# A squared-ReLU feed-forward layer on one core: the loads of w1 move from GpSimd's DMA queue to ScalarE's and SyncE's

## The chip, the cores and the metric

The kernel runs on one core of one Trainium2 chip. The metric is the device time of one execution in microseconds (us). The kernel before took 299.13 us, the median of 4 runs (298.64 to 300.1).

## The reference

```python
B, S, D, F = 1, 2048, 576, 4608      # all bf16
def reference(x, w1, b1, w2, b2):
    h = jnp.einsum("bsd,df->bsf", x, w1) + b1
    r = jnp.where(h > 0, h, 0)
    h = r * r
    return jnp.einsum("bsf,fd->bsd", h, w2) + b2
```

Two matrix products with a squared ReLU between them. The hidden dimension F is 36 tiles of 128; the model dimension D = 576 is four tiles of 128 and a rest of 64, or nine slices of 64. The 2048 rows of x are worked on in four blocks of 512.

## The kernel before, in words

**Stage A** makes the hidden layer, transposed, block by block of x. Since D is nine slices of 64, TensorE's 128 rows are used as two halves: one hidden tile contracts on rows 0 to 63 and another one on rows 64 to 127. So the 36 hidden tiles are taken in 18 *pairs* (`pairs`, line 81). The weights lie in SBUF as `w1h`: the first tile of each pair on partitions 0 to 63 (the *lower half*, h = 0), the second on 64 to 127 (the *upper half*, h = 1). A pair costs 18 matmuls (line 179, `a_part`), nine for each half, and then for each half one ScalarE instruction (line 163: bias and ReLU, PSUM to the SBUF tile `r`, of which there are four buffers) and one VectorE instruction (line 165: the square), together `evac_h`.

**Stage B** (from line 285) multiplies the hidden layer by w2, tile by tile of 128 rows of x, and stores the result. TensorE goes from A to B without a pause.

**The start.** `w1h` is large, so the loads come in the order of need.

- The first four hidden tiles (the *quads*, `qn`, and the rest rows, `qr`) are computed with 128 rows of contraction at once, for block 0 only, while `w1h` is on its way. SyncE and ScalarE each issue two tiles of x and two quads (lines 101 to 108). TensorE transposes x by itself (line 146), VectorE and ScalarE copy the transposes from PSUM to SBUF (lines 137, 139, 151), and line 194 multiplies them with the quads. Line 219 adds the rest rows `qr`. The four results lie in four PSUM banks (`bk0`) until lines 163 and 165 evacuate them (lines 223 to 226).
- Then block 0 goes over the other 16 pairs in groups of four (G = 4): *group one* is pairs 2 to 5, *group two* pairs 6 to 9, *group three* 10 to 13, *group four* 14 to 17. Pairs 0 and 1 of `w1h` are not needed before block 1.
- Group one is treated apart: its halves are loaded in two parts, even and odd slices (`w1_first`, line 121), and TensorE goes over the four pairs with the first five slices of each (lines 260 to 262) before it does the other four (lines 263 to 266). There are 8 PSUM banks: the four of `bk0` and those of the first two pairs fill them, and the third pair waits for banks that the evacuation of `bk0` frees.
- `load_w1` (line 97) loads one half of some pairs. In the kernel before, SyncE issues all lower halves and GpSimd all upper halves (lines 122 to 127 and 234): group one in two parts (320 KB and 256 KB), then one transfer of 576 KB for each further group, then 288 KB for pairs 0 and 1. GpSimd also loads the rest rows (line 113) and b1 (line 116). The small copy in line 120 makes GpSimd wait until the first tile of x is there.
- Behind w1, SyncE issues the DMA transposes of x for the blocks 1 to 3 (`load_xT`, line 232), then b2 and parts of w2. `finish_xT` (lines 255 and 256) copies two slices of a transposed block on VectorE; that of block 1 stands in the program behind pair 14 of block 0.

**What sets the order.** The schedule is manual: each engine runs its instructions, DMA issues included, in the order of the program. So a DMA issue on ScalarE that has to wait, or that takes long, holds up ScalarE's copies and evacuations behind it. The framework puts in the semaphores. In the trace, the DMAs from SyncE and ScalarE share eight completion semaphores, which go round in program order, and GpSimd's DMAs eight others; a DMA that reuses a semaphore is issued only after the DMA that had it last has landed.

Of the kernel before, what the change touches and what calls it, by code (L numbers as in the profile page):

```python
# [11 lines left out]
BF16 = mybir.dt.bfloat16  # L12
# [5 lines left out]
def kernel(  # L18
# [9 lines left out]
    nc = tc.nc  # L28
    P = 128
    H = 64  # L30
    x2 = x.flatten_outer_dims()
    out2 = out.flatten_outer_dims()
    S, D = x2.shape
    F = w1.shape[1]
    FH = F // 2
    G = 4
# [3 lines left out]
    NH = D // H  # L40
    DM = NC * P
# [8 lines left out]
    const = ctx.enter_context(tc.tile_pool(name="const", bufs=1))  # L50
# [18 lines left out]
    def early(n):  # L69
        at[0] += n  # L70
        assert at[0] <= NFT * D
        return w2_sb[:, at[0] - n:at[0]]
# [5 lines left out]
    xs = early(RT * D).rearrange("p (j c) -> p j c", c=D)  # L78
    qn = early(NC * 4 * P).rearrange("p (c f) -> p c f", c=NC)
    qr = early(2 * P)  # L80
# [10 lines left out]
    def load_x(eng, j):  # L91
        eng.dma_start(out=xs[:, j, :], in_=x_view[:, j, :])
# [4 lines left out]
    def load_w1(eng, h, j0, n, cs):  # L97
        f0 = pairs[j0][h] * P
        eng.dma_start(out=w1h[h * H:(h + 1) * H, cs, j0 * P:(j0 + n) * P], in_=w1_rows[:, cs, f0:f0 + n * P])  # L99
# [7 lines left out]
    load_x(nc.sync, 2)  # L107
    load_x(nc.scalar, 3)

    ident = const.tile([P, P], BF16, name="ident")  # L110
    make_identity(nc, ident[:])
    for h in range(2):
        nc.gpsimd.dma_start(out=qr[h * H:(h + 1) * H, :], in_=w1[DM:D, 2 * h * P:2 * (h + 1) * P])
    b1_rows = const.tile([P, P], BF16, name="b1_rows")
    nc.gpsimd.memset(b1_rows[:], 0.0)
    nc.gpsimd.dma_start(out=b1_rows[0:NFT, :], in_=b1.rearrange("(ft p) -> ft p", p=P))


    seen = const.tile([P, 1], BF16, name="seen")
    nc.gpsimd.tensor_copy(out=seen[:], in_=xs[:, 0, 0:1])  # L120
    w1_first = ((slice(0, 9, 2), slice(1, 8, 2)), (slice(1, 8, 2), slice(0, 9, 2)))
    for part in range(2):
        for h, eng in enumerate((nc.sync, nc.gpsimd)):
            load_w1(eng, h, 2, G, w1_first[h][part])
    for m in range(1, 4):
        for h, eng in enumerate((nc.sync, nc.gpsimd)):
            load_w1(eng, h, 2 + G * m, G, slice(0, NH))

    ones = nc.const_aps.tensor(1.0, [P, SB], BF16)
    wps = bank("wps")  # L130
# [4 lines left out]
    def copy_psum(eng, dst, src):  # L135
        if eng is nc.scalar:
            nc.scalar.copy(out=dst, in_=src)  # L137
        else:
            nc.vector.tensor_copy(out=dst, in_=src)  # L139

    def transpose_chunks(half, cs, engs):
        tps = [psum.tile([P, HALF], BF16, name="tp", tag="bank") for c in cs]
        for i in range(2):
            for c, tp in zip(cs, tps):
                d0 = c * P if c < NC else D - P
                nc.tensor.transpose(tp[:, i * P:(i + 1) * P], xs[:, 2 * half + i, d0:d0 + P], ident[:])  # L146
        cols = slice(half * HALF, (half + 1) * HALF)
        for c, tp, eng in zip(cs, tps, engs):
            copy_psum(eng, xT[0][:, c if c < NC else 7, cols], tp[:])
            if c == NC:  # L150
                nc.vector.tensor_copy(out=xT[0][0:H, 8, cols], in_=tp[H:P, :])
# [39 lines left out]
    def full_mm(half, c):  # L191
        cols = slice(half * HALF, (half + 1) * HALF)
        for q in range(4):
            nc.tensor.matmul(bk0[q][:, cols], lhsT=qn[:, c, q * P:(q + 1) * P], rhs=xT[0][:, c, cols],  # L194
                             start=(half == 0 and c == 0), stop=False, skip_group_check=True)
# [4 lines left out]
    full_mm(0, 0)  # L200
    transpose_chunks(0, (2,), (A,))
    full_mm(0, 1)
    transpose_chunks(0, (3,), (V,))
    full_mm(0, 2)
    transpose_chunks(1, (0, 1), (V, A))
# [2 lines left out]
    full_mm(1, 0)  # L208
    transpose_chunks(1, (2,), (A,))
    full_mm(1, 1)  # L210
    transpose_chunks(1, (3,), (V,))
    nc.tensor.transpose(b1T_ps[:], b1_rows[:], ident[:])
    full_mm(1, 2)
# [17 lines left out]
        for i in range(2):  # L231
            nc.sync.dma_start_transpose(out=xT[b][:, i * NC:(i + 1) * NC, :], in_=x2[rows, i * H:i * H + DM])

    for h, eng in enumerate((nc.sync, nc.gpsimd)):
        load_w1(eng, h, 0, 2, slice(0, NH))
    for b in range(1, NSB):
        load_xT(b)
    w2_view = w2_dram.rearrange("(ft p) d -> p ft d", p=P)
# [106 lines left out]
```

## Time and profile before

| | |
|---|---|
| median of 4 runs | 299.13 us |
| the profiled execution, its own time | 298.77 us |
| its span, first to last instruction | 297.0 us |
| TensorE matmuls, busy | 286.6 us (96%) |
| ScalarE, VectorE, GpSimd, busy | 94.9, 79.5, 8.1 us |
| HBM read, written | 11.94 MB, 2.36 MB |
| share of the chain by line: L179, L305, w1h transfers | 44%, 42%, 6% |

The page has, for each engine, the time in which it was busy; the span in 40 slices of 7.4 us each with busy tenths, TensorE's granted clock and the DMA rate; the DMA queues (q1 is SyncE's, q10 ScalarE's, q0 GpSimd's); and the chain of work that ended last, followed back from the last instruction. In lists of instructions the columns are start, duration, engine, line, operation, what it writes and reads, shapes and count, and in brackets the idle time ahead of it and who ended it. A matmul's own duration (376 ns) is longer than the distance from one to the next, because they are pipelined. In lists of DMA issues the last number is the time from the issue to the landing.

### The profile page before, as it was taken

The page shows a single profiled execution, that of the slowest core. Times are in us where ns is not written, and L with a number is a line of the kernel's source. Part 1 is how long each engine was busy: PE and PEld are TensorE (multiplying, and loading weights), DVE is VectorE, ACT ScalarE, POOL GpSimd, SP SyncE. Part 2 cuts the span into 40 slices and gives each one's busy share as a digit, 9 for nine tenths or more (in the row PEclk, how much of TensorE's full clock was granted, in tenths as well). Part 3 has the DMA queues.
Part 4 walks back from the last instruction along what each step waited for, and adds up shares of the span by engine and source line. Part 5 has one row for each costly group of instructions (what it writes and reads, how often), then busy time and mean ns, then how long its engine had stood idle before and what let it go on. Part 6 is the DMA issues. An engine that isn't in the chain of part 4 may idle for free.

```text
span 297.0 us, 4817 instructions
## 1 busy us (share of the span) xinstructions
PE 286.6 (96%) x2068; PEld 136.0 (46%) x2079; DVE 79.5 (27%) x196; ACT 94.9 (32%) x151; POOL 8.1 (3%) x19
## 2 busy tenths in 40 slices
PE   7958999999999999999999999999999999999995
PEld 3743444444444444444445444444444444444454
DVE  1541445445444454444440011000111111111111
ACT  2462666666666666666650000000000000000000
POOL 8200000000000000000000000000000000000000
PEclk9997999999999999999999999999999999999999
DMA  7999999200030000600000010000000000000000
GB/s 214 264 253 173 191 201 314 74 2 2 0 121 0 2 1 10 231 2 0 2 0 3 18 20 20 20 22 20 20 20 22 20 20 20 22 20 20 20 22 21
DMA packets 25925, 18.01 MB, mean 61 GB/s; under 512 B 14516, under 2 KB 25216, under 8 KB 25904
## 3 DMA queue, kind: packets, MB, share of 16 engines
q1 hardware_dynamic: 24416, 14.42, 19.9%
q0 software_dynamic: 912, 2.73, 3.6%
q10 hardware_dynamic: 576, 0.56, 0.6%
q8 instruction: 16, 0.26, 0.4%
q14 instruction: 5, 0.04, 0.0%
HBM read 11.94 MB, written 2.36 MB: 48 GB/s over the span
## 4 chain that ended last, share of the span: by engine, by line
PE 91%; DMA 7%; SPq 0%; issue 0%; DVE 0%
PE ph L179 44%; PE po L305 42%; DMA w1h<-in_w_dram 6%; PE pc L291 5%; DMA w_sb<-in_x_dram 1%; SPq L99 0%; DVE o_sb L307 0%
## 5 line engine op out<-in xcount | busy, mean ns | idle before, releaser
L163 ACT ACTIVATE r<-ph,b1T 128x512 bf16<-128x512 f32 x144 | 90.8, 686 | 54.8 <-PE ph L179 53.4
L179 PE MATMUL ph<-w_sb,w1h 64*128 64x512 bf16 x936 | 103.2, 380 | 4.5 <-DMA w1h<-in_w_dram 4.5
L179 PEld LDWEIGHTS <-w1h 64*128 64x128 bf16 x1260 | 64.3, 95 | 78.3 <-DMA w1h<-in_w_dram 5.8
L305 PE MATMUL po<-w_sb,hT 128*128 128x512 bf16 x423 | 92.9, 379 | 0.5
L305 PEld LDWEIGHTS <-hT 128*128 128x128 bf16 x432 | 42.2, 98 | 51.2 <-issue 0.4
L165 DVE TENSOR_TENSOR hT<-r 128x512 bf16<-128x512 bf16 x108 | 46.0, 426 | 61.2 <-ACT r L163 61.1
L307 DVE TENSOR_TENSOR o_sb<-po,b_bc 128x512 bf16<-128x512 f32 (+2 forms) x17 | 11.2, 660 | 116.7 <-PE po L305 109.7
L179 PE MATMUL ph<-xT,w1h 64*128 64x512 bf16 x324 | 35.1, 376 | 0.0
L305 PE MATMUL po<-w_sb,w1h 128*128 128x512 bf16 (+2 forms) x178 | 31.2, 336 | 0.1
L305 PEld LDWEIGHTS <-w1h 128*128 128x128 bf16 x180 | 16.2, 98 | 15.3
L165 DVE TENSOR_TENSOR w1h<-r 128x512 bf16<-128x512 bf16 x36 | 15.3, 426 | 19.6 <-ACT r L163 19.6
L291 PE MATMUL pc<-hT,w_sb 128*64 128x512 bf16 x108 | 15.7, 379 | 0.0
L291 PEld LDWEIGHTS <-w_sb 128*64 128x64 bf16 x144 | 8.1, 110 | 7.6 <-issue 0.4
L291 PE MATMUL pc<-w1h,w_sb 128*64 128x512 bf16 x36 | 7.9, 379 | 0.0
L293 ACT ACTIVATE oc<-pc,b2T 128x512 bf16<-128x512 f32 x2 | 1.4, 688 | 13.7 <-PE pc L291 13.7
L194 PE MATMUL ph<-w_sb 128*128 128x256 bf16 x32 | 4.5, 272 | 1.1 <-DMA w_sb<-in_w_dram 0.8
L301 DVE COPY o_sb<-oc 128x64 bf16<-128x64 bf16 x16 | 2.8, 172 | 9.4 <-DMA oc<-oc 9.4
L99 POOL DMA_DIRECT2D w1h<-in_w_dram x6 | 4.3, 716 | 0.0
L139 DVE COPY w_sb<-tp 128x256 bf16<-128x256 bf16 x6 | 1.7, 290 | 7.3 <-PE tp L146 7.3
L194 PEld LDWEIGHTS <-w_sb 128*128 128x128 bf16 x32 | 2.8, 97 | 1.6 <-DMA w_sb<-in_w_dram 1.3
L133 PE MATMUL wps<-const-bfloat16-1.0 128*128 128x512 bf16 x6 | 2.7, 623 | 0.8 <-PEq L329 0.8
L137 ACT COPY w_sb<-tp 128x256 bf16<-128x256 bf16 x4 | 1.5, 372 | 3.7 <-PE tp L146 3.6
(29 smaller groups left out, 15.5 us busy)
## 6 DMA issues: line engine op xcount, KB each, us to landing
w_sb<-in_w_dram SPq DMA_DIRECT2D x6, 864.0 KB, 6.4
out_dram<-o_sb SPq DMA_DIRECT2D x15, 144.0 KB, 1.7
w1h<-in_w_dram SPq DMA_DIRECT2D x3, 576.0 KB, 21.0
w1h<-in_w_dram POOLq DMA_DIRECT2D x3, 576.0 KB, 12.6
w1h<-in_w_dram SPq DMA_DIRECT2D x1, 320.0 KB, 7.4
w1h<-in_w_dram POOLq DMA_DIRECT2D x1, 320.0 KB, 7.5
w_sb<-in_x_dram ACTq DMA_DIRECT2D x2, 144.0 KB, 4.0
w_sb<-in_x_dram SPq DMA_DIRECT2D x2, 144.0 KB, 3.7
```

Source lines behind the costliest of these rows:

```text
L99: eng.dma_start(out=w1h[h * H:(h + 1) * H, cs, j0 * P:(j0 + n) * P], in_=w1_rows[:, cs, f0:f0 + n * P])
L133: nc.tensor.matmul(wps[:], lhsT=ones[:, 0:P], rhs=ones[:], start=(i == 0), stop=(i == NWARM - 1))
L137: nc.scalar.copy(out=dst, in_=src)
L139: nc.vector.tensor_copy(out=dst, in_=src)
L163: nc.scalar.activation(out=r[:], in_=bk[:], func=ACT.Relu, bias=b1T[:, ft:ft + 1], scale=1.0)
L165: nc.vector.tensor_tensor(out=hT_of(b, ft), in0=r3, in1=r3, op=ALU.mult)
L179: nc.tensor.matmul(bk[h][:], lhsT=w1h[rows, c, j * P:(j + 1) * P], rhs=xT[b][rows, place(h, c), :], start=(i == 0), stop=(i == NH - 1))
L194: nc.tensor.matmul(bk0[q][:, cols], lhsT=qn[:, c, q * P:(q + 1) * P], rhs=xT[0][:, c, cols], start=(half == 0 and c == 0), stop=False, ski ...
L291: nc.tensor.matmul(pc[h * H:(h + 1) * H, :], lhsT=w2(ft, DM, D), rhs=hT_of(2 * pr + h, ft), start=(ft == 0), stop=(ft == NFT - 1))
L301: nc.vector.tensor_copy(out=o_sb[:, DM:D], in_=o_tr[pr][:, jj, h * H:(h + 1) * H])
L305: nc.tensor.matmul(po[:, 0:e - a], lhsT=hT_of(b, ft)[:, jj, :], rhs=w2(ft, a, e), start=(ft == 0), stop=(ft == NFT - 1))
L307: nc.vector.tensor_tensor(out=o_sb[:, a:e], in0=po[:, 0:e - a], in1=b2_bc[:, a:e], op=ALU.add)
```

## The change

GpSimd no longer loads w1 or the rest rows. ScalarE's queue takes the upper halves of groups one and two, in three DMAs that stand between its copies in program order: the odd slices of group one right after its first four loads, the even slices after its second copy of a transpose, and group two after its last copy. All else goes to SyncE: the rest rows, the lower halves, and both halves of groups three and four and of pairs 0 and 1, one after the other. The copy in line 120 goes away. The bytes that are loaded and the computation are the same.

```diff
@@ after load_x(nc.scalar, 3) @@
+    def load_rest(eng, h):
+        eng.dma_start(out=qr[h * H:(h + 1) * H, :], in_=w1[DM:D, 2 * h * P:2 * (h + 1) * P])
+
+    load_rest(nc.sync, 0)
+    w1_first = ((slice(0, 9, 2), slice(1, 8, 2)), (slice(1, 8, 2), slice(0, 9, 2)))
+    load_w1(nc.scalar, 1, 2, G, w1_first[1][0])
+    load_w1(nc.sync, 0, 2, G, w1_first[0][0])
+    load_rest(nc.sync, 1)
+    load_w1(nc.sync, 0, 2, G, w1_first[0][1])
+
     ident = const.tile([P, P], BF16, name="ident")
     make_identity(nc, ident[:])
-    for h in range(2):
-        nc.gpsimd.dma_start(out=qr[h * H:(h + 1) * H, :], in_=w1[DM:D, 2 * h * P:2 * (h + 1) * P])
...
-    seen = const.tile([P, 1], BF16, name="seen")
-    nc.gpsimd.tensor_copy(out=seen[:], in_=xs[:, 0, 0:1])
-    w1_first = ((slice(0, 9, 2), slice(1, 8, 2)), (slice(1, 8, 2), slice(0, 9, 2)))
-    for part in range(2):
-        for h, eng in enumerate((nc.sync, nc.gpsimd)):
-            load_w1(eng, h, 2, G, w1_first[h][part])
-    for m in range(1, 4):
-        for h, eng in enumerate((nc.sync, nc.gpsimd)):
-            load_w1(eng, h, 2 + G * m, G, slice(0, NH))
...
     transpose_chunks(0, (2,), (A,))
     full_mm(0, 1)
+    load_w1(nc.scalar, 1, 2, G, w1_first[1][1])
     transpose_chunks(0, (3,), (V,))
...
     transpose_chunks(1, (2,), (A,))
     full_mm(1, 1)
+    load_w1(nc.scalar, 1, 2 + G, G, slice(0, NH))
+    load_w1(nc.sync, 0, 2 + G, G, slice(0, NH))
     transpose_chunks(1, (3,), (V,))
...
-    for h, eng in enumerate((nc.sync, nc.gpsimd)):
-        load_w1(eng, h, 0, 2, slice(0, NH))
+    for j0, n in ((2 + 2 * G, G), (2 + 3 * G, G), (0, 2)):
+        for h in range(2):
+            load_w1(nc.sync, h, j0, n, slice(0, NH))
     for b in range(1, NSB):
         load_xT(b)
```

## The prediction

> **What bounds the kernel now.** I read the chain that ended last first. TensorE is at its start and end; between lies one transfer, from 4.96 to 23.36 us, and nothing else is as long.
>
> ```profile
> 4.96 18.39 DMA w1h<-in_w_dram
> 23.36 0.05 issue
> 23.40 130.06 PE ph L179 x1188
> 153.47 15.66 PE pc L291 x144
> ```
>
> After it TensorE runs to the end without a hole, so what can be won lies ahead of 23.4 us. Next, the timeline from 0 to 40 us, at the DMA issues, ScalarE's start and the matmuls of line 179:
>
> ```profile
> 2.15 0.46 ACTq L92 DMA_DIRECT2D w_sb<-in_x_dram  x1
> 2.63 1.28 ACT L137 ACT_TABLE_LOAD   x1 [2.63 <-issue]
> ...
> 4.84 0.60 PE L194 MATMUL ph<-w_sb 128*128 128x256 bf16 x4
> 5.04 0.37 ACT L137 COPY w_sb<-tp 128x256 bf16<-128x256 bf16 x1 [0.66 <-PE tp L146]
> ...
> 10.61 2.42 ACT L163 ACTIVATE r<-ph,b1T 128x512 bf16<-128x512 f32 x4 [1.47 <-PE ph L219]
> ...
> 11.01 8.06 PE L179 MATMUL ph<-w_sb,w1h 64*128 64x512 bf16 x72 [0.22 <-DMA w1h<-in_w_dram]
> ...
> 23.40 16.97 PE L179 MATMUL ph<-w_sb,w1h 64*128 64x512 bf16 x140 [4.33 <-DMA w1h<-in_w_dram]
> ```
>
> The 72 matmuls of the first group start at 11.01. The pace of a pair is 1.943 us (ScalarE's pairs of line 163 at 31.12, 33.07, 35.01), so a matmul costs 1.943/18 = 0.108 us and the second group could start at 11.01 + 72 x 0.108 = 18.78. It starts at 23.40: a **gap of 4.62 us**. Which half is late? The issues around 5.3 us, with their time to landing:
>
> ```profile
> w1h<-in_w_dram SPq DMA_DIRECT2D x1, 576.0 KB, 18.4
> w1h<-in_w_dram POOLq DMA_DIRECT2D x1, 576.0 KB, 10.3
> ```
>
> The upper half of the second group (GpSimd) lands at 5.11 + 10.3 = 15.4, the lower (SyncE) at 4.96 + 18.4 = 23.4. The queues from 12 to 20 us (packets, MB, share of 16 engines; q0 is GpSimd's, q1 SyncE's) say why:
>
> ```profile
> q0 software_dynamic: 439, 1.61, 79.0%
> q1 hardware_dynamic: 436, 0.44, 26.0%
> ```
>
> As many packets of each queue, but GpSimd's are nearly four times as large: its groups three and four pass SyncE's group two. Last, the stretches, whose last three figures are TensorE's granted clock, the DMA share and GB/s:
>
> ```profile
> 3.00:6.00 3.00, 2.28 (x20) 1.55 (x18) 1.07 (x4) 1.66 (x3) 2.86 (x6) 1.00 1.01 298
> 12.00:20.00 8.00, 7.07 (x66) 5.72 (x63) 3.58 (x9) 4.64 (x9) 0.00 (x0) 1.00 1.06 258
> 24.00:28.00 4.00, 4.00 (x26) 1.53 (x22) 0.43 (x1) 1.26 (x2) 0.00 (x0) 0.57 1.24 185
> ```
>
> The third line's clock of 0.57: the gap also costs (1 - 0.57) x 4 = 1.7 us. Cross-check: 1188 matmuls x 0.108 = 128.2, the chain has 130.06: 1.8 us, taken.
>
> **Gain if the gap goes:** 4.62 + 1.8 = 6.4 us.
>
> **Part 1, order of arrival.** Up to the second group go x and the first quads (1.11 MB), the rest rows (0.07) and two groups (1.18 each): 3.54 MB, now with nothing of groups three and four beside the lower half, and two hardware queues whose packets are alike. By 6.0 us 1.19 MB had moved (271 GB/s from 2 to 3, then 298). The other 2.35 MB take 9.1 us at the 258 GB/s of 12 to 20 us: drained at 15.1. A landing lags, since the DMA engines do not finish together: SyncE's row had started as many packets as reach through its second group at 20.3, and landed at 23.4; for its odd rows of group one 10.6 against 12.5. With a lag of 1.9 to 3.1 the second group lands at 17.0 to 18.2. TensorE wants it at 18.86 (part 2): **no gap**.
> Here the Trainium skill speaks against the change ("SBUF — State Buffer", sections on the port swizzle and on two DMAs for both halves): a transfer to partitions 0 to 63 reaches half of the ports (196 GB/s measured there), and a second one to the other half adds only 6%. The trace agrees on one half alone: 196 GB/s from 22.5 to 25 us, SyncE's queue only. It doesn't agree on two: 258 with both. By the rule (208) the second group would drain at 6.0 + 11.3 = 17.3, land by 20.4 at worst, and leave 1.5 us of the gap; I take the row.
> Groups three, four and the first two pairs now go one half after another, so at 196: 15.1 + 6.0 + 3.1 = 24.2 for group three (wanted at 18.86 + 7.77 = 26.6), 30.2 for four (wanted at 34.4), last packet of w1 at 30.1 (the last landed at 29.7 before). The transposes behind them landed at 32.4 and 35.7, so some 36.1; their first reader, the VectorE copy of line 255, ran at 44.54, now at 38.2. Hidden, with 2 us left; behind that copy wait VectorE's squares, and behind those four r buffers and the PSUM banks, so another 3 us pass before TensorE feels it.
>
> **Part 2, ScalarE's queue.** The framework's eight semaphores go round over SyncE's and ScalarE's DMAs in program order, and a ninth waits for the first to land (SyncE's first w1 DMA waited 1.0 us for x). So ScalarE's first w1 DMA, tenth in that order, waits for the second x load: 0.74 + 2.8 = 3.54. It issues in 0.65 (SyncE's of this size: 0.73 and 0.61), to 4.2. Behind it: the table load (1.28, to 5.5) and both first copies (0.37 each), which end at 5.92 and 6.3 instead of 4.37 and 5.41. TensorE waits for them: its block at 4.84 starts at 5.95, the next transposes end at 6.85, and the block that waited until 6.38 for a quad starts at 6.85: **+0.47**. All that follows up to the four matmuls of line 219 (10.19 to 10.62) shifts alike, and line 179 can start at 11.09 instead of 11.01, where 0.39 was a wait for w1 that goes (lower even rows: 0.92 MB of SyncE's queue at half of 298 from 2.1, plus lag, 9.8). So +0.08; were the table loaded ahead of the DMA, it is -0.39. I take +0.08.
> The second w1 DMA waits for the last quad (1.66 + 5.1 = 6.8) and ends at 7.5; the next copy isn't due before 8.1. It brings the upper even rows by some 12, as before (11.9). The third follows the last copy (9.24 to 9.61) and ends at 10.35; line 163 starts at 11.08. Both hidden.
>
> **Part 3, SyncE and GpSimd.** Two rest loads ahead on SyncE put its first w1 DMA from 3.53 to 4.1, its second, behind a quad's semaphore, to 6.4: inside part 1's rates, since 0.6 MB is queued then. GpSimd loses 4.25 + 1.21 us of issues and the small copy, none on the chain; b1 comes earlier, read at 9.11 only.
>
> **Sum:** 4.62 + 1.8 - 0.08 = 6.3 us. The profiled execution took 298.77 (span 297.0): 292.4, span 290.7. The median of the runs is 0.36 above it: **292.8 us**.
>
> **The unknown cost: a blocked ScalarE.** An issue lasts longer when its row is full: SyncE's took 1.18, 2.22 and 8.78 us at the end, with some 1880 and 1850 of its packets issued and not done as the last two ended. In the new kernel SyncE reaches that at 9 to 10 us, in group three's upper and group four's lower half, just when ScalarE wants its third DMA out (9.6). The skill ("Perfetto Trace Analysis", the HWDGE DMA instruction) has a descriptor generator shared by the issuing sequencers and locked for one. The nearest row is against a costly lock: at 0.74 us SyncE and ScalarE issued side by side in 0.38 and 0.41; but no row there was full. By the row it costs nothing (taken); by the rule, between nothing and all of SyncE's blocked time:
> - held for one issue: group four's lower half is in when 3520 - 1850 = 1670 packets are done; 1094 at 9.5, then 150 per us: 13.3. ScalarE's evacuation starts at 14.0 instead of 11.1; the third pair needs the banks that it frees, and waits from 13.25 to 15.3: 2.0 us lost. 294.8 us.
> - held until SyncE has w1 out: 5248 - 1850 = 3400 done, at 196 per us at 21.3. Below.
>
> **Rivals.**
> *Part of the gap stays*, by that single hold, or by 196 to 208 GB/s with the longest lag (second group at 20.4 to 21.2, 1.5 to 2.3 us): 293.6 to 297, the upper end with the half clock again. For it: less than 1 us of margin in part 1.
> *Slower:* ScalarE's third DMA stays shut out until 21.3. Its evacuation starts at 22.0, the third pair at 23.2, and 52 matmuls later (5.6 us) it is 28.8; the upper half lands at about 29 too. The second group starts 5.6 us later than before: 299.13 + 5.6 = 304.7. It decides from a third issue that ends after 16.6 us (16.6 + 1.2 + 5.6 = 23.4). For it: that issue stands just where SyncE's row fills; against: SyncE itself pauses between issues.
> *The change doesn't do what it says:* the second group still lands near 23, as the engine that lagged 3.1 us lags more. 297.6 to 300.6, no change; I see no reason in the rates.
>
> **How the numbers follow.** No gap 0.55 (292.0 to 293.6); part of it stays 0.28 (to 297); no change 0.05; slower 0.12. What this measurement can tell from no change is 0.5%, 1.5 us. The first two are faster, 0.83; with edges of both, same 0.04 and slower 0.13. The range reaches over the first two cases, 291.8 to 297.0, and leaves out less than 2 in 10.
>
> **What would show it.** Line 179 starts near 11.1 and runs on at 0.108 per matmul, no clock below 1.0 up to 40 us, both halves of group two landed by 18.2, GB/s near 258 to 15 us and near 196 after. ScalarE's first copy at 5.5. Wrong: a third issue on ScalarE of over 2 us, line 163 after 11.5, or a wait of line 179 on w1h.

## The result, and the profile after

The kernel after took 298.69 us, the median of 35 runs (296.48 to 301.51), beside 299.64 us for the kernel before in 56 runs (297.98 to 302.65). The ratio is 0.9964, with a 95% interval of 0.9949 to 0.9978: 0.4% faster, within the 0.5% that was named as no change. 292.8 us was predicted. (The ratios here and below leave out runs over 1.5% above the fastest of their kernel; medians and ranges take in all.)

The chain of work that ended last, after:

```profile
6.45 9.50 DMA w1h<-in_w_dram
15.95 0.05 issue
16.00 137.72 PE ph L176 x937
```

A transfer of w1 still stands ahead of TensorE's long stretch. It is another one: the DMA issued at 6.45 us is ScalarE's second of w1, the even slices of the upper half of group one. What TensorE waits for has moved forward, from group two to group one. The timeline of the kernel after shows the step (columns as before: start, duration, engine, line, operation, and in brackets the idle time ahead):

```profile
3.74 0.68 ACTq L99 DMA_DIRECT2D w1h<-in_w_dram  x1
...
5.74 0.65 ACT L134 COPY w_sb<-tp 128x256 bf16<-128x256 bf16 x2
...
6.45 0.63 ACTq L99 DMA_DIRECT2D w1h<-in_w_dram  x1
...
9.73 0.60 ACTq L99 DMA_DIRECT2D w1h<-in_w_dram  x1
...
10.80 1.24 PE L176 MATMUL ph<-w_sb,w1h 64*128 64x512 bf16 x9
...
16.00 8.22 PE L176 MATMUL ph<-w_sb,w1h 64*128 64x512 bf16 x52 [3.96 <-DMA w1h<-in_w_dram]
```

Line 176 (line 179 before) starts at 10.80 and stops after nine matmuls: the lower half of one pair has had its first five slices and the upper half four, its odd ones; the fifth, slice 8, is among the even slices. 10.80 + 9 x 0.108 = 11.77, so TensorE stands until 16.00: a **gap of 4.23 us** in place of the 4.62 that went. The issues of the kernel after, just at 6.43 to 6.45 us and at 9.7 us (the last number is the time from issue to landing):

```profile
w1h<-in_w_dram SPq DMA_DIRECT2D x1, 576.0 KB, 8.7
w1h<-in_w_dram ACTq DMA_DIRECT2D x1, 320.0 KB, 9.5
...
w1h<-in_w_dram ACTq DMA_DIRECT2D x1, 576.0 KB, 13.1
```

SyncE's lower half of group *two*, issued 0.02 us earlier, lands at 15.1; ScalarE's even slices of group *one* at 15.95; ScalarE's upper half of group two at 9.73 + 13.1 = 22.8. The queues of the kernel after, from 8 to 10 us (q1 is SyncE's, q10 ScalarE's; packets, MB, share of 16 engines), and then from 16 to 21 us:

```profile
q1 hardware_dynamic: 490, 0.45, 102.4%
q10 hardware_dynamic: 18, 0.02, 3.2%
...
q10 hardware_dynamic: 536, 0.55, 58.3%
q1 hardware_dynamic: 547, 0.54, 55.6%
```

From 8 to 10 us ScalarE's queue moves next to nothing, although its DMA was out by 7.1 us; from 16 us on both move alike. The stretches of the kernel after (last three figures: granted clock, DMA share, GB/s):

```profile
12.00:16.00 4.00, 0.04 (x3) 0.01 (x2) 1.35 (x4) 0.94 (x2) 0.00 (x0) 0.77 1.14 234
16.00:21.00 5.00, 5.00 (x24) 1.75 (x26) 0.00 (x0) 0.00 (x0) 0.00 (x0) 0.50 1.14 219
```

After the gap the clock is 0.50 for 5 us, and 1.00 from then on: 2.5 us lost, where before lost 1.8. (The half clock lasted 6.83 us, from 14.14 to 20.97, and 1.9 of it fell into the gap; before it lasted 3.41 us, from 24.17 to 27.58, all of it behind the gap.) Gap and clock make 6.7 us, before 4.62 + 1.8 = 6.4; line 179 started 0.2 us earlier. So stage B should start about as before, and it does: 153.72 beside 153.47. What was won and lost in the first 25 us cancels. That it cancels so nearly is chance: two different transfers made the two gaps. The end from VectorE's last addition to the end of the span was 2.58 us instead of 3.03 in these two executions, which makes up for it: 298.57 us (span 296.8) beside 298.77 (297.0). What the rest of the 0.95 us between the medians is made of was not found.

### The profile page after: what moved, and what is told of

It reads as the page before. It is cut to its first block, busy times and chain, and to the rows that moved or that the text cites. A ratio compares the mean times of both kernels' runs of the same rounds, so it can differ in the third digit from the quotient of the medians.

```text
span 296.8 us, 4811 instructions
## 1 busy us (share of the span) xinstructions
PE 287.2 (97%) x2068; PEld 131.6 (44%) x2079; DVE 79.5 (27%) x196; ACT 94.7 (32%) x151; POOL 2.6 (1%) x10
## 4 chain that ended last, share of the span: by engine, by line
PE 93%; DMA 5%; ACTq 0%; issue 0%; DVE 0%
PE ph L176 46%; PE po L306 42%; PE pc L292 5%; DMA w1h<-in_w_dram 3%; DMA w_sb<-in_x_dram 1%; ACTq L95 0%; ACTq L92 0%; DVE o_sb L308 0%
## 5 line engine op out<-in xcount | busy, mean ns | idle before, releaser
L176 PEld LDWEIGHTS <-w1h 64*128 64x128 bf16 x1260 | 59.9, 95 | 82.8 <-DMA w1h<-in_w_dram 4.5
L308 DVE TENSOR_TENSOR o_sb<-po,b_bc 128x512 bf16<-128x512 f32 (+2 forms) x17 | 11.2, 660 | 116.6 <-PE po L306 109.7
L143 PE MATMUL tp<-ident,w_sb 128*128 128x128 bf16 x20 | 2.4, 232 | 0.1
## 6 DMA issues: line engine op xcount, KB each, us to landing
w1h<-in_w_dram ACTq DMA_DIRECT2D x1, 576.0 KB, 13.1
```

The source lines that it names most:

```text
L176: nc.tensor.matmul(bk[h][:], lhsT=w1h[rows, c, j * P:(j + 1) * P], rhs=xT[b][rows, place(h, c), :], start=(i == 0), stop=(i == NH - 1))
L308: nc.vector.tensor_tensor(out=o_sb[:, a:e], in0=po[:, 0:e - a], in1=b2_bc[:, a:e], op=ALU.add)
```

## Experiments

The question: why did ScalarE's two late DMAs land so late, when they were issued in time? Three theories stand in the expectations below. **T1**: the DMAs of SyncE and of ScalarE are taken in the order in which they were issued, whatever queue they are in. **T2**: SyncE's queue is served first. **T3** is neither of them: in in_order, that halves loaded one after another are too slow in any order; in hold_lower2, that ScalarE's DMA was merely issued too late. All times are compared with the kernel before on the same chip.

**in_order.** Against the kernel after, ScalarE keeps only the first of its three DMAs. SyncE issues the other two, in the order of need.

```diff
     load_w1(nc.sync, 0, 2, G, w1_first[0][1])
+    load_w1(nc.sync, 1, 2, G, w1_first[1][1])
...
-    load_w1(nc.scalar, 1, 2, G, w1_first[1][1])
...
-    load_w1(nc.scalar, 1, 2 + G, G, slice(0, NH))
     load_w1(nc.sync, 0, 2 + G, G, slice(0, NH))
+    load_w1(nc.sync, 1, 2 + G, G, slice(0, NH))
```

> The changed kernel, but ScalarE loads only the odd slices of group one's upper half; its other two w1 DMAs go by SyncE, each at its place in the order of need. Theory 1 (SyncE's and ScalarE's DMAs are made ready one after the other, in the order of issue, and only as the queues drain; so ScalarE's second w1 DMA stood behind SyncE's group two): the even rows of the upper half follow the lower odd rows, land near 13.4 instead of 15.95, group two lands near 20; two short waits of 1 to 2 us in all, no long half clock, 293 to 295 us. Theory 2 (the DMA engines serve SyncE's ring first as long as it has packets): the same here. Theory 3 (halves one after another are simply too slow, 196 GB/s, whatever the order): group two lands after 22, and the time stays at 297 to 299 us.

Measured: 293.39 us (292.74 to 293.85), ratio 0.9799 (0.9769 to 0.9830). Timeline of in_order, line 177 being the same matmul, and the issue of the even slices:

```profile
10.86 1.24 PE L177 MATMUL ph<-w_sb,w1h 64*128 64x512 bf16 x9
...
13.03 32.33 PE L177 MATMUL ph<-w_sb,w1h 64*128 64x512 bf16 x298 [0.93 <-DMA w1h<-in_w_dram]
```

```profile
w1h<-in_w_dram SPq DMA_DIRECT2D x1, 320.0 KB, 6.0
```

The even slices were issued at 7.00, *later* than in the kernel after, and landed 6.0 us later at 12.98, three us *earlier*. The upper half of group two, issued at 8.32, took 10.5 us and landed at 18.8. The only stop left was 1.2 us at group one, with the clock at 1.00. So the gain that was forecast is there to be had, and the late landings of the kernel after are no matter of their time of issue alone. T1 and T2 both allow this run, since within one queue they say the same; of T3, that halves in turn are too slow falls here.

**hold_lower2.** The kernel after, with one more instruction: GpSimd copies one column into the place where SyncE's lower half of group two will be written, once a copied piece of x is there. The load overwrites the column; it only has to wait for it, and so is issued at 8.54 us instead of 6.43, behind ScalarE's even slices. (Those went out earlier too in this run, at 5.57 instead of 6.45, and so ahead of SyncE's odd slices at 6.04.)

```diff
+    nc.gpsimd.tensor_copy(out=w1h[0:H, 0, (2 + G) * P:(2 + G) * P + 1], in_=xT[0][0:H, 1, HALF:HALF + 1])
     load_w1(nc.scalar, 1, 2 + G, G, slice(0, NH))
     load_w1(nc.sync, 0, 2 + G, G, slice(0, NH))
```

> The changed kernel, but SyncE's group-two lower half (and all behind it) waits for a one-column GpSimd copy that waits for ScalarE's third copy of a transpose, so that it is issued at about 8.3 us instead of 6.43, after ScalarE's second w1 DMA (6.45) and not just ahead of it. Theory 1 (made ready in the order of issue): ScalarE's second w1 DMA lands at 11.5 to 12.5 us instead of 15.95, the wait ahead of group one's third slice goes, and a wait for the upper half of group two (which is still issued behind group three) comes near 19 to 22 us; total within 1% of the changed kernel. Theory 2 (SyncE's ring is served first while it has packets): SyncE has packets queued without a break up to 30 us here too, so it lands at 15 us or later. Theory 3 (late issue only): it lands where it did, 15 to 16.

Measured: 294.36 us (two runs, 293.77 and 294.94), ratio 0.9833 (0.9784 to 0.9883). Issue of the even slices in hold_lower2, its timeline, and then its queues from 14 to 16 us:

```profile
w1h<-in_w_dram ACTq DMA_DIRECT2D x1, 320.0 KB, 6.2
```

```profile
10.86 8.15 PE L176 MATMUL ph<-w_sb,w1h 64*128 64x512 bf16 x73
...
21.69 23.48 PE L176 MATMUL ph<-w_sb,w1h 64*128 64x512 bf16 x216 [2.69 <-DMA w1h<-in_w_dram]
```

```profile
q10 hardware_dynamic: 374, 0.38, 100.2%
q1 hardware_dynamic: 58, 0.05, 12.7%
```

With SyncE's DMA 2 us later, ScalarE's even slices land at 5.57 + 6.2 = 11.8 instead of 15.95, and the gap at group one is gone, as T1 has it and neither T2 nor T3. (Their own earlier issue can't be the reason alone: in in_order they were issued at 7.00 and landed at 12.98.) T2 falls also with the last two lines: from 14 to 16 us ScalarE's queue had the engines nearly alone, while SyncE had had two halves of group three waiting since 9.2 and 9.9. The records of the single packets, counted as done by queue, show the order of issue itself (a half of group two has 576 packets, 1 KB each):

```text
us      q1 (SyncE)  q10 (ScalarE)   what mostly moves from then to the next row
 9.0        957         911         ScalarE's even slices (issued 5.57), SyncE's odd ones (6.04)
11.0       1219        1088         SyncE's lower half of group two (8.54)
14.0       1728        1102         ScalarE's upper half of group two (9.00)
16.0       1785        1463         SyncE's group three (9.20) and the rest of that half
18.0       2070        1645         SyncE's group three
21.0       2650        1664         
```

The upper half of group two was all but done at 18 us; its last 19 packets came until 20.6, so it landed at 21.6 and left a gap of 2.9 us, with the clock at 1.00. A tail of this kind is what the prediction counted as lag. The total missed: it had been expected within 1% of the kernel after and was 1.3% below it by the ratios. The upper half of group two was issued just ahead of group three (9.00 and 9.20), not behind it as expected.

**probe.** in_order, with two additional small loads (16 KB of x, into a tile that nobody reads): one from ScalarE and one from GpSimd, while SyncE's queue is full.

```diff
+            if (j0, h) == (2 + 3 * G, 0):
+                nc.scalar.dma_start(out=probes[0][:], in_=x_view[:, 0, 0:H])
+    seen = const.tile([P, 1], BF16, name="seen")
+    nc.gpsimd.tensor_copy(out=seen[:], in_=hT[0][:, 3, 0:1])
+    nc.gpsimd.dma_start(out=probes[1][:], in_=x_view[:, 0, 0:H])
```

> The kernel with all but one w1 DMA on SyncE in order of need, and two probes of 16 KB each (128 rows of 128 bytes of x into a tile that nobody reads): one from ScalarE behind its evacuation of the quads (near 13 to 15 us), one from GpSimd behind the square of the fourth quad (near 13.5 to 16 us). SyncE has several w1 DMAs issued by then. ScalarE has no other DMA outstanding. Theory 1 (made ready in the order of issue with SyncE's): ScalarE's probe lands 5 us or more after its issue, GpSimd's, which is made ready elsewhere, within 4. Theory 2 (SyncE's ring is served first): both land late, by 5 us or more. Theory 3 (neither): ScalarE's lands within 3 to 4 us.

Measured: 293.18 us, one run. Issues of probe, then its queues from 13 to 18 us, then its timeline at the two engines' issues:

```profile
probe<-in_x_dram ACTq DMA_DIRECT2D x1, 16.0 KB, 8.1
...
probe<-in_x_dram POOLq DMA_DIRECT2D x1, 16.0 KB, 7.8
```

```profile
q1 hardware_dynamic: 1124, 1.12, 112.3%
```

```profile
10.94 3.26 SPq L99 DMA_DIRECT2D w1h<-in_w_dram  x1
...
12.48 0.34 ACTq L239 DMA_DIRECT2D probe<-in_x_dram  x1
```

ScalarE issued its probe in 0.34 us in the middle of an issue on which SyncE was held for 3.26 us: the issue isn't blocked, the *transfer* is late. Its first packets moved at 18.5, 6.0 us after the issue; those of GpSimd's probe at 21.6, 6.3 us after. In between SyncE's queue alone moved 1.3 to 1.4 MB. That GpSimd's DMA waits as well was against T1 as it stood, which had only the two others in one order; T2 had forecast both, but had fallen with hold_lower2.

**before_hold.** The kernel before, where GpSimd reads a column of the lower half of group two, so waits for it to land, and only then loads its group three.

```diff
+            if m == 2 and h == 1:
+                nc.gpsimd.tensor_copy(out=seen[0:H, :], in_=w1h[0:H, 0, (2 + G) * P:(2 + G) * P + 1])
             load_w1(eng, h, 2 + G * m, G, slice(0, NH))
```

> The kernel before, but GpSimd waits, ahead of its upper half of group three, for the landing of SyncE's lower half of group two (a one-element copy that reads it). If what bounded the kernel before was GpSimd's larger packets passing SyncE's, as the prediction has it: the lower half of group two lands at 17.5 to 20 us instead of 23.4, the gap shrinks from 4.6 to 0 to 1.5 us and the half clock goes with it: 294 to 296 us. If the lower half was slow for another reason, the landing stays at 22 or later and the time within 1 us of before.

Measured: 308.59 us (305.26 to 312.88), ratio 1.0262 (1.0164 to 1.0361): a miss. The held DMA among the issues, and the timeline, of before_hold:

```profile
w1h<-in_w_dram POOLq DMA_DIRECT2D x1, 576.0 KB, 22.1
```

```profile
12.34 14.85 PE L181 MATMUL ph<-w_sb,w1h 64*128 64x512 bf16 x136 [0.65 <-DMA w1h<-in_w_dram]
...
39.89 5.43 PE L181 MATMUL ph<-w_sb,w1h 64*128 64x512 bf16 x28 [12.70 <-DMA w1h<-in_w_dram]
```

One half of it came as expected: the lower half of group two landed at 4.72 + 12.4 = 17.2 instead of 23.4, and TensorE ran through group two. So the prediction's reading of the gap before, that GpSimd's later loads pass SyncE's group two, is confirmed. But GpSimd's held DMA, issued at 17.76, moved its first packets at 24.5, when 1.10 MB of SyncE's had gone, then had to share with SyncE's transposes, and landed at 39.9, where TensorE stood 12.7 us. A load that is held joins the line behind what was issued meanwhile.

**swap_order.** in_order with two of SyncE's loads exchanged: the even slices of the upper half ahead of the odd ones of the lower, since TensorE wants them first.

```diff
     load_rest(nc.sync, 1)
+    load_w1(nc.sync, 1, 2, G, w1_first[1][1])
     load_w1(nc.sync, 0, 2, G, w1_first[0][1])
-    load_w1(nc.sync, 1, 2, G, w1_first[1][1])
```

> As the kernel in order of need, but SyncE issues the even rows of group one's upper half ahead of the odd rows of its lower half, since slice 8 of the upper half is wanted at the fifth step and the odd rows only at the sixth. Theory 1 (made ready in the order of issue): the even rows land near 11.6 instead of 13.0, the wait of 0.9 to 1.2 us at group one goes, a wait of up to 0.5 us at group two may come; 292.0 to 293.2 us, up to 1.2 below the kernel in order of need. Theory 2 (SyncE's ring first): the same. Theory 3 (halves one after another are too slow): no gain, 293.4 or more.

Measured: 293.08 us (291.91 to 293.38), ratio 0.9795 (0.9763 to 0.9826). Timeline of swap_order:

```profile
11.53 33.83 PE L177 MATMUL ph<-w_sb,w1h 64*128 64x512 bf16 x309
```

No wait for w1 is left; data came at 201 GB/s from 12 to 20 us. In this execution the start itself came 0.7 us later, behind a load of x, so the profile doesn't show the gain over in_order, and the intervals don't part the two.

**even_by_sync.** One part of that repair alone, against the kernel after: SyncE loads all even slices of group one, as in swap_order, but the upper half of group two stays with ScalarE, as in the kernel after.

```diff
     load_rest(nc.sync, 1)
+    load_w1(nc.sync, 1, 2, G, w1_first[1][1])
     load_w1(nc.sync, 0, 2, G, w1_first[0][1])
...
-    load_w1(nc.scalar, 1, 2, G, w1_first[1][1])
```

> One part of the change alone, for ScalarE's late loads: group one as in the kernel with the swapped order, the upper half of group two by ScalarE after its last copy (near 9.7), as in the changed kernel. SyncE has its lower half of group two and both halves of group three out by then. Theory 1 (made ready in the order of issue): ScalarE's first packets come at 15 to 16.5, the half lands at 21 to 23; no wait at group one, a wait of 2.5 to 4 us at group two and up to 3 us of half clock: 295.5 to 299 us. Theory 2 (SyncE's ring is served first while it has packets): the half lands after 25, 299 us or more. Neither at work: it lands by 18.5, 292 to 293 us.

Measured: 300.54 us (299.05 to 301.43), ratio 1.0035 (1.0001 to 1.0069). Timeline, issues, and queues from 18 to 22 us, of even_by_sync:

```profile
12.36 8.15 PE L177 MATMUL ph<-w_sb,w1h 64*128 64x512 bf16 x73
...
26.07 19.10 PE L177 MATMUL ph<-w_sb,w1h 64*128 64x512 bf16 x156 [5.57 <-DMA w1h<-in_w_dram]
```

```profile
w1h<-in_w_dram ACTq DMA_DIRECT2D x1, 576.0 KB, 15.5
```

```profile
q1 hardware_dynamic: 373, 0.38, 56.0%
q10 hardware_dynamic: 372, 0.38, 55.8%
```

The gap is back at group two: 12.36 + 73 x 0.108 = 20.24, so 5.8 us. ScalarE's DMA, issued at 10.50, moved its first packets at 17.9, after 1.43 MB of SyncE's; from there the queues shared equally, and it landed at 26.0. T1's figures were missed (first packets 15 to 16.5, landing 21 to 23, 295.5 to 299 us). The landing and the time are as late as T2 had them, but equal shares are not what a queue that is served first would give. Nor did T1 hold to the letter: of what SyncE had issued before 10.50, 0.49 MB had not begun when ScalarE's packets moved. (That TensorE began group one only at 12.36 has another cause: four matmuls of line 192 before it took 1.01 to 1.06 us, beside 0.60 in the kernel after, as at half clock; a part of the 300.5 is that.) So both of ScalarE's late DMAs have to go, and the kernel after hid the second one's lateness behind the first's.

**probe_shallow.** probe, with SyncE's groups three and four held back by a copy of GpSimd, so that less is outstanding when the probes are issued.

```diff
+    nc.scalar.dma_start(out=probes[0][:], in_=x_view[:, 0, 0:H])
+    seen = const.tile([P, 1], BF16, name="seen")
+    nc.gpsimd.tensor_copy(out=seen[:], in_=hT[0][:, 3, 0:1])
+    nc.gpsimd.dma_start(out=probes[1][:], in_=x_view[:, 0, 0:H])
+    nc.gpsimd.tensor_copy(out=w1h[0:H, 0, (2 + 2 * G) * P:(2 + 2 * G) * P + 1], in_=hT[0][0:H, 3, 0:1])
```

> The probe kernel with a short queue: SyncE's groups three and four wait until GpSimd has issued its probe (a one-column copy behind the square of the fourth quad), so that when ScalarE's probe goes out (near 12.5) SyncE has only group two ahead of it, and the same for GpSimd's (near 14 to 15.5). Theory 1 (made ready in the order of issue, and GpSimd's held by the same backlog in a way not known): both probes land sooner than the 8.1 and 7.8 us of the deep queue, ScalarE's in 4 to 6 us, GpSimd's in 3 to 5. If a probe's delay is nothing but the load on the DMA engines, both stay at 7 to 8 us, since packets flow at the same rate.

Measured: 292.54 us, one run. GpSimd's, issued with about 0.5 MB outstanding, took 4.7 us, as expected. ScalarE's took 7.1, more than the 4 to 6 expected and within what the rival (nothing but busy DMA engines, 7 to 8) had forecast, because I had misjudged what was in the queue: 1.1 MB of group two were outstanding at its issue at 11.04, and 1.01 MB of them went before its first packets at 15.65. Against the rival stand GpSimd's 4.7 us on the same busy engines, and that most of the 7.1 is a wait of 4.6 in which no packet of the probe moved. Up to here, the wait goes with the bytes that are ahead.

**swap_pieces.** swap_order, with the halves of groups two to four and of pairs 0 and 1 cut in two (slices 0 to 4 and 5 to 8) and lower and upper pieces in turn, to have both halves of the partitions written at once.

```diff
-    load_w1(nc.sync, 0, 2 + G, G, slice(0, NH))
-    load_w1(nc.sync, 1, 2 + G, G, slice(0, NH))
+    for cs in (slice(0, 5), slice(5, NH)):
+        for h in range(2):
+            load_w1(nc.sync, h, 2 + G, G, cs)
...
     for j0, n in ((2 + 2 * G, G), (2 + 3 * G, G), (0, 2)):
+      for cs in (slice(0, 5), slice(5, NH)):
         for h in range(2):
-            load_w1(nc.sync, h, j0, n, slice(0, NH))
+            load_w1(nc.sync, h, j0, n, cs)
```

> As the swapped order, but every later transfer of a half is cut in two (slices 0 to 4 and 5 to 8), and SyncE issues lower and upper pieces in turn. If both halves of the partitions in flight together are faster than one after the other, as before (258 against 196 GB/s), the rate from 12 to 20 us rises from some 210 to 230 GB/s or more and group two lands by 18; time 0 to 0.8 us below the swapped order. If the ports make no difference within one queue, the rate stays at 200 to 220, and the time within 0.5 us of the swapped order.

Measured: **291.92 us** (291.61 to 293.09), ratio 0.9773 (0.9739 to 0.9807), the shortest median here. Timeline of swap_pieces, and its stretch from 12 to 20 us:

```profile
10.76 34.53 PE L177 MATMUL ph<-w_sb,w1h 64*128 64x512 bf16 x318
```

```profile
12.00:20.00 8.00, 8.00 (x77) 5.48 (x74) 3.92 (x10) 5.03 (x10) 0.00 (x0) 1.00 1.14 218
```

TensorE starts at 10.76 and has no wait for w1 at all. The rate went from 201 to 218 GB/s, 8% more, in one execution of each; the 230 that had been expected if the halves help each other was not reached. By then TensorE no longer waits for it, so this says little about the time; the intervals of swap_order and swap_pieces overlap.

**gp_backlog.** The kernel before with the backlog on GpSimd's queue alone: SyncE's lower halves of groups two to four are held until a copy of GpSimd, and ScalarE issues a probe meanwhile.

```diff
-        for h, eng in enumerate((nc.sync, nc.gpsimd)):
-            load_w1(eng, h, 2 + G * m, G, slice(0, NH))
+        load_w1(nc.gpsimd, 1, 2 + G * m, G, slice(0, NH))
...
+    nc.scalar.dma_start(out=probe[:], in_=x_view[:, 0, 0:H])
+    load_w1(nc.gpsimd, 1, 0, 2, slice(0, NH))
+    nc.gpsimd.tensor_copy(out=w1h[0:H, 0, (2 + G) * P:(2 + G) * P + 1], in_=hT[0][0:H, 3, 0:1])
+    for m in range(1, 4):
+        load_w1(nc.sync, 0, 2 + G * m, G, slice(0, NH))
+    load_w1(nc.sync, 0, 0, 2, slice(0, NH))
```

> The kernel before with the backlog on GpSimd's queue only: GpSimd issues its upper halves as before, SyncE's lower halves of the groups two to four and of pairs 0 and 1 wait for a one-column GpSimd copy behind the square of the fourth quad (near 13.5 us), and ScalarE issues the 16 KB probe behind its evacuation of the quads (near 12.5), when SyncE has nothing outstanding and GpSimd three transfers of 576 KB. If the backlog of any queue holds a later DMA of every other queue (the work is taken in the order of issue), the probe lands 5 us or more after its issue, as with SyncE's backlog (8.1). If it is SyncE's and ScalarE's own making of descriptors that holds, or the packets of queues are taken in turn, it lands within 4 us. The kernel itself is slower than before, since SyncE's lower half of group two starts 9 us later: 305 us or more.

Measured: 300.52 us, one run, beside 300.92 in one run of the kernel before on the same chip; 305 or more had been expected. Issues of gp_backlog, and its queues from 12 to 17 us (q0 is GpSimd's):

```profile
probe<-in_x_dram ACTq DMA_DIRECT2D x1, 16.0 KB, 11.2
```

```profile
q0 software_dynamic: 281, 1.03, 102.0%
q1 hardware_dynamic: 11, 0.01, 1.0%
q10 hardware_dynamic: 7, 0.00, 0.2%
```

SyncE had almost nothing outstanding and ScalarE's probe, issued at 10.53, still moved its first packets only at 17.0, when 1.41 MB had gone, 1.35 of it GpSimd's. SyncE's own DMA, issued at 13.43, began at about 19.3, after 1.21 MB. So it is neither SyncE's queue that is favoured nor something that only SyncE and ScalarE share: a backlog on any of the three queues holds what others issue later (ScalarE's held SyncE's group three in hold_lower2).

## Why the prediction was wrong

**What bounds the kernel** was right: the gap at group two, its 4.6 us, the half clock behind it, and GpSimd's later loads as the cause (before_hold moved the landing to 17.2). The size was right too: in_order, with a stop of 1.2 us, takes 293.4 and swap_pieces, with none, 291.9 us, on both sides of the 292.8 that were forecast for a kernel with no gap.

**Part 2 held the step that failed**: "It brings the upper even rows by some 12, as before (11.9)". This was costed by the row of before, where that transfer is issued early, with little ahead of it. In the kernel after it is issued at 6.45, 0.02 us behind SyncE's lower half of group two, and lands at 15.95. The prediction looked at when the DMA is issued and whether the issue holds ScalarE up, and not at what the other queue has issued before it. By the packet records, a few packets moved from 9.2 and the bulk from 10.4, when SyncE's odd slices (issued at 5.77) were done; then they shared the engines with SyncE's group two. Its forecast landing stood just at the time when TensorE wants it (11.8 to 12), so there was no margin to take up the error.

**Part 1 had the same fault**: "two hardware queues whose packets are alike", sharing from the issue on. They share equally, but only from when both have begun (16 us in the kernel after; 536 and 547 packets from 16 to 21 us). So group two was not drained at 15.1: its upper half began at 16.0 and landed at 22.8, against 17.0 to 18.2 forecast. Even with group one in time, the gap at group two would have stayed, as even_by_sync shows. The rate was too high as well: 237 GB/s from 6.0 to 15.1 us, the stretch of the sum, 234 from 12 to 16 and 219 from 16 to 21, against the 258 taken from the trace of before and the 208 estimated from the Trainium skill's rule ("SBUF — State Buffer", on two DMAs for both halves). The measured rates lie between. Rate was not what decided: at 203 GB/s in_order reached the forecast time, because its transfers came in the order of need.

**The start** was right: ScalarE's first copy at 5.74 (5.55 forecast), and line 179 at 10.80, between the two values that were given: 11.09, which was taken, and 10.62 (11.01 - 0.39).

**The unknown cost**, ScalarE blocked in its third issue, was nothing, the value taken: the issues took 0.68, 0.63 and 0.60 us, and in probe ScalarE's took 0.34 us while SyncE was held for 3.26. The lock of which the skill's page speaks ("Perfetto Trace Analysis", DMA Instruction — HWDGE) doesn't show here beyond that. So the slower rival, built on it, fell. It asked what a full queue does to the issuing engine; what a full queue did was to hold the other engine's transfer.

**The rivals.** The time ended within the third one, "the second group still lands near 23", 297.6 to 300.6; the second group did land at 22.8. Its reason, an engine that lags more, is not what made it so, and the stop was not there but one group earlier. The prediction saw "no reason in the rates" for it, rightly: the reason is in the order.

**Part 3** held: the transposes were covered, no wait of VectorE reached TensorE, and GpSimd's lost work gave nothing. The **half clock** was put at 1.8 us for a gap of 4.6; a gap of 4.2 now cost 2.5. Equal gaps needn't cost the same: the half clock lasted 3.41 us before and 6.83 now.

Open: why the kernel after is still 0.95 us ahead by the medians when the two profiles differ by 0.2. And where the DMAs wait, and why the wait stops growing near 1.4 MB: ScalarE's held probe began its first 16 packets within 0.12 us in probe and 0.34 in gp_backlog, which fits one place ahead of the DMA engines as well as lists of the single engines that are equally full.

## What to carry to other kernels

Order all DMAs that are in flight together, on whatever queues, by when they are needed, and reckon that a late DMA begins only when what was issued before it has gone: here up to about 1.4 MB, some 6 us. (Behind more than that it began with 0.5 to 0.65 MB of the earlier ones still to go, so the whole backlog is the safe figure, not the exact one.) A second queue then brings no sooner landing; issuing all of w1 but one early DMA from one engine, in order of need, beat the two queues by 5 us. When a stop is to be removed, look for the transfer whose margin is smallest in the *new* order, which need not be the one that stopped the old kernel.

## What the runs showed of the hardware

**A DMA waits for what other queues have issued before it, up to about 1.4 MB.** From the records of single packets (MB; the last column is what the other queue had issued earlier and had not begun when the held DMA's first packets moved):

```text
kernel         DMA (queue)                     issued  first packets  others moved  left
hold_lower2    even slices (ScalarE)             5.57      8.0           0.31        0.06
after          even slices (ScalarE)             6.45     10.4           0.78        0.43
after          upper half, group two (ScalarE)   9.73     16.0           1.08        0.65
even_by_sync   the same (ScalarE)               10.50     17.9           1.43        0.49
probe          16 KB (ScalarE)                  12.48     18.5           1.33        0.58
probe          16 KB (GpSimd)                   15.29     21.6           1.39        0.50
probe_shallow  16 KB (ScalarE)                  11.04     15.65          1.01        0.09
gp_backlog     16 KB (ScalarE)                  10.53     17.0           1.41        0.61
gp_backlog     lower half, group two (SyncE)    13.43     19.3           1.21        0.17
before_hold    upper half, group three (GpSimd) 17.76     24.5           1.10        -
```

(ScalarE's own earlier DMA moved another 0.23, 0.20 and 0.33 MB in the first three rows. In the second, what is left is SyncE's lower half of group two, issued 0.02 us before. A DMA whose issue was still under way isn't counted as left; in the last row SyncE was issuing a transpose all the while.) With up to 1.4 MB ahead (others moved and left together), nearly all of it went first: 0.06 to 0.17 MB was left, the twin of the second row aside. With 1.7 to 2.0 MB ahead, 0.5 to 0.65 MB was overtaken. So T1 holds as far as about 1.4 MB and not beyond.

The Trainium skill says that an engine takes turns between the queues that it has work for, packet by packet ("DMA: Bandwidth & Descriptors", Queues, rings and completion order), and that DMAs of different issuing engines interleave (Issuing engines are not separate DMA queues). By the first, a held probe should begin after one turn of the other queue: with the page's typical 9 to 17 descriptors in a packet, taken as rows of 1 KB, that is 0.15 to 0.28 MB over 16 engines, an estimate; with its ceiling of 64 it is 1.05 MB. It took 1.33 to 1.41 MB, and the probes landed after 8.1, 7.8 and 11.2 us. Turns are what the trace shows among DMAs that have begun, as in the equal shares of the kernel after from 16 us on. For one that hasn't, it shows a wait.

**Pieces of both halves in turn on one queue** moved 218 GB/s from 12 to 20 us where whole halves moved 201 (one execution of each): 8%, near the 6% that the skill has for two DMAs at once ("SBUF — State Buffer", on two DMAs for both halves). The 258 of the kernel before, with SyncE's and GpSimd's queues at once, is more than either.
